# Two mask additions moved from TensorE to VectorE, block means of v in products of their own, and new queues

## Chip, core and metric

The kernel runs on 1 core of one Trainium2 chip. The metric is device time of one execution in microseconds, the median of several runs. The engines are TensorE (PE, with its weight loads as PEld), VectorE (DVE), ScalarE (ACT), GpSimd (POOL) and SyncE (SP), which here issues all transfers. Each engine runs its own queue in order and waits on semaphores for the others.

## What is computed

An attention over a narrow band and block summaries, followed by a GELU MLP, with 4 batches, 8 heads, 768 positions, head dimension 64; d_model 512, d_ff 2048. Inputs and output are f32; the MLP weights arrive as f64.

```python
k_sum = k.reshape(B, H, nb, block, D).max(axis=3)        # block = 32, nb = 24
v_sum = v.reshape(B, H, nb, block, D).mean(axis=3)
scores_l = scale * np.matmul(q, k.transpose(0, 1, 3, 2))
mask_l = np.abs(pos[:, None] - pos[None, :]) < window    # window = 16
scores_s = scale * np.einsum('bhsd,bhnd->bhsn', q, k_sum) + np.log(block)
scores_all = np.concatenate([np.where(mask_l, scores_l, -1e9), scores_s], axis=-1)
a = np.exp(scores_all - scores_all.max(-1, keepdims=True))
a = a / (a.sum(-1, keepdims=True) + 1e-09)
x = np.matmul(a, np.concatenate([v, v_sum], axis=2))     # then heads side by side
h = x @ w_in
out = 0.5 * h * (1 + erf(h / sqrt(2))) @ w_out
```

## The kernel before

The positions are cut into 12 chunks of 256 (`CH`). Attention works in 24 units: one unit is 256 positions of 4 heads (two pairs), so two units feed one chunk of the MLP. A unit's scores are 8 tiles of 128 x 128: the rows are 64 positions of two tiles, the columns a window of 96 keys, 24 block summaries and 8 unused columns.

Units 0 to 5 (batch 0, `WIDE`) are the f32 units, in which the start-up consists. Their products run in f32, straight from what is loaded: `scores` multiplies q by windows of k (`kp0`, 96 columns) and by block maxima (`ks32`, 24 columns), which `prep_k` takes on DVE out of a load of two pairs of heads. The band mask and log(32) are put into PSUM ahead of the scores by `f_mask`, eight products with unit matrices, and the scores accumulate on them. `maximum_p` (DVE) takes row maxima out of PSUM, `exponent_p` (ACT) the exponentials. Units 0 to 2 (`TURNED`) also turn the probabilities on PE in f32 (`p_turn`, kept by ACT's `p_keep`), and multiply them by v in f32 (`values`, 16 products of 64 x 64, in which the block means stand as 24 further rows of v). The means come from `sum_vt` (six products with an indicator) and `mean_vt` (ACT), and `s_load_vs` (ACT) copies them into rows 96 to 119 of each unit's v. From unit 3 on probabilities and v are split in two f16 parts, and the probabilities are turned by DMA (`turn`).

The MLP splits each operand into a high and a low f16 part (three products for one). `w_in` is loaded in 8 column tiles, `w_out` in 8 row tiles, all as f64. Three DVE instructions (`wh_bits`, `wi_bits`, `wo_bits`; the first for half a tile) put together the f32 value, ACT makes the high part (`wi_hi`, `wo_hi`) and DVE the low part (`wi_lo`, `wo_lo`). `take_hi` and `take_lo` do the same for x. `phase1` is a tile of x @ w_in for one chunk (`phase1h` half of its depth), `gelu`, `g_hi`, `g_lo` work on its result, `phase2` is the second product; from chunk 4 on Strassen-like sums of blocks (`product`, `s_product`) take their place. The last PE steps are `s_last`, the last ones on ACT and SP `s_end`.

The order is written out by hand: `ORDER` is a list of some 1,650 steps, each of which issues its instructions on one engine, so the order of each engine's queue is the order of its steps in the list. `warm` steps are products of ones that feed nothing. Of the four banks and rings that steps share, those that matter here are the accumulators `ps_s` (scores of all units but unit 1) and `ps_v` (values), the five PSUM banks, and the single f32 v buffer of units 0, 2 and 3.

Of the kernel before, what the change touches and what calls it, by code (L numbers as in the profile page):

```python
# [80 lines left out]
wh_bits 6 0 2, wh_bits 1 0 0, warm 1 1, f_mask 2, scores 2, maximum_p 2, p_turn 0 1, p_turn 0 0, sum_vt 0,
wi_hi 6 0, exponent_p 2, p_keep 0 1, mean_vt 0, p_keep 0 0, s_load_vs 0, recip 1, wh_bits 1 0 1, p_norm 1,
wi_lo 6 0, wi_bits 4 0, wh_bits 1 0 2, wi_hi 1 0, wi_lo 6 1, wi_bits 4 1, recip 2, wi_bits 4 2, s_norm 2,
p_turn 1 0, p_turn 1 1, f_mask 3, scores 3, values 0, p_keep 1 1, p_keep 1 0, take_hi 0, maximum_p 3, wi_lo 1 0,
sum_vt 1, p_turn 2 1, p_turn 2 0, mean_vt 1, exponent_p 3, s_load_vs 1, wi_bits 0 0, wi_bits 0 1, take_lo 0,
wi_bits 0 2, phase1h 0 6 0, phase1h 0 1 0, f_mask 4, values 1, wi_bits 2 0, wi_bits 2 1, load_q 4, fetch_wh 7 1,
recip 3, wi_hi 4 1, wi_hi 4 0, wi_hi 0 0, wi_bits 2 2, wi_hi 2 0, take_hi 1, wh_bits 7 1 0, scores 4, load_q 5,
load_v 2, fetch_wh 7 0, fetch_w_in 3, fetch_w_out 4, p_keep 2 1, p_keep 2 0, s_load_vs 2, wi_hi 2 1, wi_lo 4 0,
wh_bits 7 1 1, take_lo 1, phase1h 0 4 0, wi_lo 4 1, wi_lo 2 0, p_norm 3, phase1h 0 6 1, values 2, load_v 3,
s_p_hi 3, turn 3 0, wi_lo 0 0, maximum_p 4, wi_lo 2 1, wh_bits 7 0 0, wi_bits 3 0, wh_bits 7 0 1, p_lo 3, take_hi 2,  # L90
# [20 lines left out]
phase2 0 0, phase2 0 1, phase2 1 0, phase2 1 1, phase2 1 5, phase2 1 4, phase2 0 4, phase2 0 5, phase2 0 3,
phase2 0 2, phase2 1 2, phase2 0 6, phase2 0 7, values 5, k_sums 1 1, take_hi 5, scores 6, take_lo 5, add_mask 6,
maximum 6, s_q_hi 8, store 0 0, store 0 1, s_k_hi 7, k_lo 7, phase2 1 6, phase2 1 3, scores 7, q_lo 8, prep_v 1 0,
load_k 8, load_v 6, fetch_v 1 1, exponent 6, recip 6, s_q_hi 9, s_k_hi 8, s_norm 6, s_p_hi 6, add_mask 7, q_lo 9,
k_lo 8, maximum 7, exponent 7, phase1 2 0, phase1 2 4, scores 8, phase1 2 5, phase2 1 7, load_k 9, load_q 10,
gelu 2 4, gelu 2 0, gelu 2 5, g_hi 2 5, s_q_hi 10, s_k_hi 9, g_hi 2 4, fetch_k 2 0, turn 6 0, prep_v 1 1, load_vs 6,
put 0 1, load_q 11, load_k 10, p_lo 6, add_mask 8, recip 7, t_add 1 0, maximum 8, prep_k 2 0, t_add 0 1, phase1 2 1,
phase1 2 3, v_hi 6, store 1 1, gelu 2 1, s_k_hi 10, gelu 2 3, g_hi 2 1, k_lo 9, scores 9, s_q_hi 11, turn 6 1,
v_lo 6, p_norm 7, g_lo 2 5, prep_k_end 2 0, g_lo 2 1, values 6, g_hi 2 0, take_hi 6, s_p_hi 7, g_hi 2 3, exponent 8,
fetch_v 3 0, load_v 7, fetch_v 3 1, load_k 11, put 1 1, load_vs 7, turn 7 0, phase1 2 7, phase1 2 6, gelu 2 6,  # L120
g_lo 2 0, take_lo 6, phase2 2 1, phase1 2 2, prep_v 3 0, q_lo 10, g_lo 2 3, phase2 2 0, t_add 1 1, p_lo 7,
add_mask 9, g_lo 2 4, turn 7 1, k_lo 10, t_add 2 1, recip 8, s_k_hi 11, v_hi 7, v_lo 7, k_lo 11, gelu 2 7,
store 1 0, s_norm 8, values 7, take_hi 7, scores 10, gelu 2 2, s_p_hi 8, phase2 2 5, take_lo 7, maximum 9,
load_q 12, load_v 8, put 0 0, prep_v 3 1, q_lo 11, t_add 1 2, p_lo 8, exponent 9, s_q_hi 12, q_lo 12, recip 9,
p_norm 9, fetch_k 2 1, turn 8 0, load_k 12, load_vs 8, turn 8 1, fetch_v 2 0, phase1 3 3, gelu 3 3, add_mask 10,
g_hi 2 2, g_lo 2 2, g_hi 2 7, v_hi 8, phase1 3 1, gelu 3 1, s_p_hi 9, phase1 3 2, k_sums 2 0, g_hi 3 1, g_hi 2 6,
v_lo 8, load_v 9, load_q 13, put 1 0, load_k 13, phase1 3 0, values 8, scores 11, p_lo 9, turn 9 0, load_vs 9,
phase1 3 5, phase2 2 2, phase2 2 4, phase2 2 3, t_add 0 2, maximum 10, gelu 3 2, s_k_hi 12, k_lo 12, t_add 0 3,
exponent 10, prep_k 2 1, add_mask 11, maximum 11, s_k_hi 13, x_take 8, g_lo 2 7, k_lo 13, exponent 11, v_hi 9,
g_lo 2 6, recip 10, p_norm 10, prep_k_end 2 1, phase2 2 6, v_lo 9, recip 11, gelu 3 0, s_p_hi 10, g_hi 3 0,  # L130
s_norm 11, sx_hi 2 0, s_q_hi 13, g_hi 3 2, turn 9 1, fetch_v 2 1, values 9, prep_v 2 0, prep_v 2 1, x_take 9,
store 2 0, load_k 14, load_q 14, load_v 10, load_vs 10, turn 10 0, g_lo 3 0, p_lo 10, scores 12, phase1 3 4,
phase1 3 7, phase1 3 6, turn 10 1, load_k 15, t_add 2 2, g_lo 3 1, sx_lo 2 0, t_add 1 3, g_lo 3 2, q_lo 13,
gelu 3 5, g_hi 3 5, v_hi 10, g_hi 3 3, g_lo 3 3, k_sums 2 1, s_k_hi 14, gelu 3 4, g_hi 3 4, gelu 3 6, add_mask 12,
v_lo 10, product 2 0 1, phase2 3 1, values 10, scores 13, s_q_hi 14, t_hi 0 0, s_p_hi 11, p_lo 11, t_hi 0 1,
# [1207 lines left out]
```

## Time and profile before

| | |
|---|---|
| median of 3 runs | 549.82 us (549.75 to 550.33) |
| the profiled execution's own time | 549.92 us |
| its span, first to last instruction | 548.1 us |
| busy: PE, DVE, ACT | 539.9, 452.8, 429.7 us |
| mean granted TensorE clock | 0.999 of full speed |
| DMA moved | 74.90 MB, 137 GB/s over the span |

Times of the trace count from the start of the span; the rest of the execution (1.8 us) lies around it. A busy time is a sum over records, and one engine's records may overlap, so two starts that follow on one another say what an instruction takes of its engine's time.

### The profile page before, as it was taken

The page shows a single profiled execution, that of the slowest core. Times are in us where ns is not written, and L with a number is a line of the kernel's source. Part 1 is how long each engine was busy: PE and PEld are TensorE (multiplying, and loading weights), DVE is VectorE, ACT ScalarE, POOL GpSimd, SP SyncE. Part 2 cuts the span into 40 slices and gives each one's busy share as a digit, 9 for nine tenths or more (in the row PEclk, how much of TensorE's full clock was granted, in tenths as well). Part 3 has the DMA queues.
Part 4 walks back from the last instruction along what each step waited for, and adds up shares of the span by engine and source line. Part 5 has one row for each costly group of instructions (what it writes and reads, how often), then busy time and mean ns, then how long its engine had stood idle before and what let it go on. Part 6 is the DMA issues. An engine that isn't in the chain of part 4 may idle for free.

```text
span 548.1 us, 14376 instructions
## 1 busy us (share of the span) xinstructions
PE 539.9 (98%) x6049; PEld 401.0 (73%) x6049; DVE 452.8 (83%) x638; ACT 429.7 (78%) x1009; POOL 0.8 (0%) x9
## 2 busy tenths in 40 slices
PE   9799999999999999999999999999999999999997
PEld 4688884447877675687665787756677888888886
DVE  5999999999989988989879674885889999987411
ACT  3998967859999998899999999998877656655300
POOL 0000000000000000000000000000000000000000
PEclk9999999999999999999999999999999999999999
DMA  8997675597989645472554643434330000100021
GB/s 329 408 381 195 212 242 166 172 287 198 246 224 215 174 122 157 115 200 60 121 153 109 166 80 76 105 99 118 62 69 1 1 20 1 39 2 1 11 67 59
DMA packets 73633, 74.90 MB, mean 137 GB/s; under 512 B 46944, under 2 KB 52960, under 8 KB 73568
## 3 DMA queue, kind: packets, MB, share of 16 engines
q1 hardware_dynamic: 73568, 73.99, 47.2%
q8 instruction: 47, 0.77, 0.6%
q14 instruction: 18, 0.15, 0.1%
HBM read 54.90 MB, written 6.29 MB: 112 GB/s over the span
## 4 chain that ended last, share of the span: by engine, by line
PE 95%; DMA 2%; DVE 2%; issue 0%; ACT 0%; SPq 0%; ACTq 0%
PE bank L1017 27%; PE bank L1080 10%; PE bank L1081 10%; PE bank L1082 10%; PE bank L1194 10%; PE ps_v L923 4%; PE bank L976 4%; PE bank L989 4%; PE bank L977 4%; PE bank L978 4%; PE ps_s L793 3%; PE ps_s L1194 2%; PE ps_v L1194 2%; DMA stage<-in_w_in_dram 1%; PE ps_s L775 1%; DMA w_out_l<-in_kp_first_dram 1%
## 5 line engine op out<-in xcount | busy, mean ns | idle before, releaser
L1080 PE MATMUL bank<-w_out_h,gh 128*128 128x512 f16 x256 | 97.1, 379 | 0.0
L1081 PE MATMUL bank<-w_out_l,gh 128*128 128x512 f16 x256 | 97.0, 379 | 0.0
L1082 PE MATMUL bank<-w_out_h,gl 128*128 128x512 f16 x256 | 97.0, 379 | 0.0
L1017 PEld LDWEIGHTS <-w 128*128 128x128 f16 x640 | 62.5, 98 | 9.3
L1017 PEld LDWEIGHTS <-w_in 128*128 128x128 f16 x576 | 55.9, 98 | 9.2
L1067 DVE SCALAR_TENSOR_TENSOR gl<-g,gh 128x512 f16<-128x512 f32 x76 | 51.4, 685 | 5.9 <-ACT gh L1063 5.9
L833 ACT ACTIVATE s<-s,s_top 128x128 f32<-128x128 f32 x144 | 55.6, 390 | 0.3 <-DVE s_top L810 0.2
L1029 DVE TENSOR_TENSOR g<-bank,late 128x512 f32<-128x512 f32 x48 | 32.9, 685 | 20.4 <-PE bank L1017 9.5
L1063 ACT ACTIVATE gh<-g 128x512 f16<-128x512 f32 x76 | 45.9, 624 | 2.0 <-PE bank L1081 1.4
L1082 PEld LDWEIGHTS <-gl 128*128 128x128 f16 x256 | 25.0, 98 | 30.2
L1017 PE MATMUL bank<-x,w_in 128*128 128x256 f16 x384 | 47.1, 273 | 0.0
L1080 PEld LDWEIGHTS <-gh 128*128 128x128 f16 x256 | 25.0, 98 | 26.7
L1081 PEld LDWEIGHTS <-gh 128*128 128x128 f16 x256 | 25.1, 98 | 26.2
L1017 PE MATMUL bank<-stage,w 128*128 128x256 f16 x320 | 43.6, 273 | 0.0
L1017 PE MATMUL bank<-x,w 128*128 128x256 f16 x320 | 43.4, 273 | 0.0
L1023 ACT ACTIVATE late<-bank 128x512 f32<-128x512 f32 x48 | 28.1, 588 | 19.2 <-PE bank L1017 14.7
L976 PE MATMUL bank<-x,w_in 128*128 128x256 f16 x144 | 39.3, 273 | 0.0
L978 PE MATMUL bank<-x,w_in 128*128 128x256 f16 x144 | 39.3, 273 | 0.0
L977 PE MATMUL bank<-x,w_in 128*128 128x256 f16 x144 | 39.3, 273 | 0.0
L1049 ACT ACTIVATE g<-g 128x512 f32<-128x512 f32 x48 | 29.4, 624 | 9.1 <-DVE g L1029 9.0
L870 ACT ACTIVATE s<-s,s_rec 128x128 f32<-128x128 f32 x104 | 31.7, 390 | 2.1 <-DVE s_rec L848 2.1
L1049 ACT ACTIVATE g<-bank 128x512 f32<-128x512 f32 x48 | 27.9, 590 | 6.5 <-DVE gl L1067 2.1
(242 smaller groups left out, 1242.1 us busy)
## 6 DMA issues: line engine op xcount, KB each, us to landing
v<-in_vw_dram SPq DMA_DIRECT2D x23, 512.0 KB
stage<-in_w_out_dram SPq DMA_DIRECT2D x8, 1024.0 KB
q<-in_qd_dram SPq DMA_DIRECT2D x24, 256.0 KB
k<-in_kd_dram SPq DMA_DIRECT2D x18, 320.0 KB
out_dram<-ot SPq DMA_DIRECT2D x22, 256.0 KB
stage<-in_vb_dram SPq DMA_DIRECT2D x6, 768.0 KB
stage<-in_kp_dram SPq DMA_DIRECT2D x4, 768.0 KB
stage<-in_w_in_dram SPq DMA_DIRECT2D x4, 512.0 KB
```

The source lines that it names most:

```text
L833: nc.scalar.activation(self.s32[:, gs], score[:, ss], AF.Exp, bias=self.top[:, g : g + 1], scale=scale, accum_out=self.den[:, g : g + 1],)
L976: nc.tensor.matmul(dst, wh, xh, start=(k == 0), stop=False)
L977: nc.tensor.matmul(dst, wh, xl, start=False, stop=False)
L978: nc.tensor.matmul(dst, wl, xh, start=False, stop=(k == NCC - 1))
L1017: nc.tensor.matmul(dst, l, r[:, k], start=(first and e == 0 and k == 0 and n == 0), stop=(k == KH - 1 and n == 2), skip_group_check=True,)
L1049: nc.scalar.activation(g, h, AF.Gelu, scale=1.0 / (SC_X * SC_WI))
L1063: nc.scalar.activation(gh, two(g_slot(c, i)), AF.Copy, scale=SC_G)
L1067: nc.vector.scalar_tensor_tensor(out=gl, in0=two(g_slot(c, i)), scalar=SC_G, in1=gh, op0=ALU.mult, op1=ALU.subtract)
L1080: nc.tensor.matmul(t, gh[:, f, js], w_out_h[:, f, :], start=(n == 0), stop=False)
L1081: nc.tensor.matmul(t, gh[:, f, js], w_out_l[:, f, :], start=False, stop=False)
L1082: nc.tensor.matmul(t, gl[:, f, js], w_out_h[:, f, :], start=False, stop=(n == NFC - 1))
L1194: nc.tensor.matmul(acc[:, t * NH : (t + 1) * NH], a[:, f, js], b[:, f], start=(first and j == 0 and t == 0 and f == 0 and n == 0), stop=(f ...
```

## The change

Units 4 and 5 get no `f_mask`: their scores start fresh in PSUM, and DVE adds a mask in f32 (`add_mask`, from a new tile `wide_sb` of 128 KB, loaded by `load_wide`), takes the maximum from SBUF (`maximum` in place of `maximum_p`) and ACT the exponentials from SBUF. Their summary products write 32 columns in place of 24, so that the unused columns are defined. In units 0 to 2 the block means are no longer rows of v: `values_wide` multiplies 96 rows of v by the probabilities as before (16 products), and adds four f32 products of the 24 means with 256 columns each; `s_load_vs` of these units goes, and that of units 3 to 5 stays. v of batch 0 is loaded with 96 rows (384 KB) in place of 128 (512 KB). k of batch 0 comes in four loads, a pair of heads each (400 KB), in place of two of 864 KB, and its block maxima in four DVE steps of half the size. In `scores_wide` the eight window products of a pair come first, then its eight summary products. ORDER is a new list over the whole program.

The engines' instruction counts that differ: PE loses 8 products of 64 x 512 and 8 of 64 x 4 x 24 and gains 12 of 64 x 256; DVE gains 2 additions of 128 x 1024 and loses 2 scalings of 128 x 8, and takes k's maxima in 4 instructions for 2; ACT loses 3 copies of 24 x 1024 and 4 of its 26 table loads, and takes 16 of its exponentials from SBUF.

```diff
-fetch_k 0 0, load_m16, load_q 0, fetch_k 0 1, load_eye, load_q 1, fetch_wh 6 1, fetch_wh 1 1, warm 2 9, warm 3 3,
...
+fetch_kq 0, fetch_kq 1, load_m16, load_q 0, fetch_kq 2, fetch_kq 3, fetch_wh 1 0, load_q 1, prep_kq 0, warm 0 12,
...
-    SP = S + 96
+    SP = S + 2 * WINDOW
...
+    wide_sb = room_h[:, NTT * DM : NTT * DM + 2 * P]
...
+    def load_wide():
+        nc.sync.dma_start(out=wide_sb, in_=mask[:, NMT * TQ + P + NIND :])
...
     def setup():
         nc.gpsimd.memset(ones, 1.0)
+        nc.gpsimd.memset(v32[0][WIDE_SUM:], 0.0)
+        nc.gpsimd.memset(nc_pad, 0.0)
...
-        if b == 0:
-            nc.sync.dma_start(out=kp0[:, rs], in_=kp_first[rs].rearrange("r p s -> p r s"))
-            kst[b, g] = kp0[:, rs, WINDOW : WINDOW + S]
-            return
...
+    def fetch_kq(r):
+        nc.sync.dma_start(out=kp0[:, r], in_=kp_first[r])
+
+    def prep_kq(r):
+        nc.vector.tensor_reduce(
+            out=ks32[:, r], in_=kp0[:, r, WINDOW : WINDOW + S].rearrange("p (n j) -> p n j", j=BLOCK), axis=AX.X, op=ALU.max,
+        )
...
         def load_v(self):
-            nc.sync.dma_start(out=self.v32, in_=vw[self.u].rearrange("p (n j) -> p n j", j=D))
+            rows = slice(0, P if self.b else WIDE_SUM)
+            nc.sync.dma_start(out=self.v32[rows], in_=vw[self.u, rows].rearrange("p (n j) -> p n j", j=D))
...
         def scores_wide(self):
             r0, c0 = self.h0 // 2, self.t0 * TQ
+            sums, pad = ks_flat, 0 if self.masked else P - WIDE_SUM - NBLK
             pse = [self.ps(e) for e in range(2)]
-            for g in range(NG // 2):
-                r, t2 = g // 2, g % 2
-                for part in range(2):
+            for r in range(NR):
+                for part, t in ((part, t) for part in range(2) for t in range(CT)):
+                    g, c = r * CT // 2 + t // 2, t % 2
                     for e in range(2):
-                        for c in range(2):
...
+                            start=not self.masked, stop=(not self.masked or g == NG // 2 - 1 and part == 1),
...
         def add_mask(self):
-            m = self.masks(mask_sb, 2 * NR)
+            m = wide_sb[:, : 2 * P if self.edge else P].unsqueeze(1).broadcast_to([P, UH * (1 if self.edge else 2), 2 * P if self.edge else P]) if self.wide else self.masks(mask_sb, 2 * NR)
...
+        def values_wide(self):
+            for i in range(NR * CT):
+                r, t = divmod(i, CT)
+                for e in range(2):
+                    nc.tensor.matmul(
+                        ps_v[e * D : (e + 1) * D, i * TQ : (i + 1) * TQ], self.v32[:WIDE_SUM, (t * NR + r) * 2 + e, :],
+                        pt32[:WIDE_SUM, e * QCOLS + i * TQ : e * QCOLS + (i + 1) * TQ], start=(i == 0), stop=False, skip_group_check=True,
+                    )
+            rows = slice(WIDE_SUM, WIDE_SUM + NBLK)
+            for r in range(NR):
+                for e in range(2):
+                    h, cs = self.h0 + 2 * r + e, slice(r * CH, (r + 1) * CH)
+                    nc.tensor.matmul(
+                        ps_v[e * D : (e + 1) * D, cs], vm0[rows, h * D : (h + 1) * D],
+                        pt32[rows, e * QCOLS + r * CH : e * QCOLS + (r + 1) * CH], start=False, stop=True, skip_group_check=True,
+                    )
```

Three places show how the queues change. First SP at the very start of the program: the loads of before (kp_first is k of batch 0, mask 128x664 the f16 mask tile, mask 128x128 the unit matrix, qd a unit's q, w_in a half or a whole column tile, vt the v from which the means come).

```order
L546 DMA w_out_l<-in_kp_first_dram 128x2x864
L373 DMA misc<-in_mask_dram 128x664
L672 DMA q_0_83<-in_qd_dram 128x512
L546 DMA w_out_l<-in_kp_first_dram 128x2x864
L379 DMA misc<-in_mask_dram 128x128
L672 DMA q_1_84<-in_qd_dram 128x512
L456 DMA stage<-in_w_in_dram 128x2x512
L456 DMA gl_107<-in_w_in_dram 128x2x512
L672 DMA q_0_83<-in_qd_dram 128x512
L456 DMA stage<-in_w_in_dram 128x2x512
L456 DMA gl_107<-in_w_in_dram 128x2x512
L592 DMA w_out_h<-in_vt_dram 128x2x768
```

And of the change, the same place (a mask row of 128x272 is the unit matrix with the indicator):

```order
L558 DMA w_out_l<-in_kp_first_dram 128x800 x2
L374 DMA misc<-in_mask_dram 128x664
L684 DMA q_0_83<-in_qd_dram 128x512
L558 DMA w_out_l<-in_kp_first_dram 128x800 x2
L462 DMA gl_107<-in_w_in_dram 128x2x512
L684 DMA q_1_84<-in_qd_dram 128x512
L462 DMA stage<-in_w_in_dram 128x2x512
L684 DMA q_0_83<-in_qd_dram 128x512
L462 DMA stage<-in_w_in_dram 128x2x512
L383 DMA misc<-in_mask_dram 128x128
L377 DMA w_out_h<-in_mask_dram 128x272
L604 DMA w_out_h<-in_vt_dram 128x2x768
```

k comes in four pieces, of which two stand ahead of the first q load, and with 800 columns each for 864. The first half tile of weights to come is now one of tile 1 (into gl) and the second one of tile 6 (into stage), before the other way round; each goes one place up against the third q load, which stays behind two of them. The unit matrix, which `p_turn` reads, goes from fifth to tenth place.

Second, DVE from the reciprocals of unit 0 to the maximum of unit 2 (two rows into s_top_98 and their scaling are the maxima of unit 1; rows of 128x512 or 2x256 are weight steps). Before, with the maximum of unit 2 as the last row:

```order
L402 TENSOR_SCALAR w_1_76<-gl_107 128x512
L407 SCALAR_TENSOR_TENSOR w_1_76<-gl_107,w_1_76 128x512
L402 TENSOR_SCALAR w_2_77<-stage 128x512
L411 SCALAR_TENSOR_TENSOR w_1_76<-gl_107,w_1_76 128x512
L821 TENSOR_REDUCE s_top_98<-bank_66 128x4
L821 TENSOR_REDUCE s_top_98<-bank_67 128x4
L825 TENSOR_SCALAR s_top_98<-s_top_98 128x8
L407 SCALAR_TENSOR_TENSOR w_2_77<-stage,w_2_77 128x512
L421 SCALAR_TENSOR_TENSOR w_in_72<-w_1_76,w_in_72 128x2x256
L411 SCALAR_TENSOR_TENSOR w_2_77<-stage,w_2_77 128x512
L402 TENSOR_SCALAR w_1_76<-gl_107 128x512
L810 TENSOR_REDUCE s_top_95<-ps_s 128x8
```

Of the change, from the same step to the same:

```order
L408 TENSOR_SCALAR w_2_77<-stage 128x512
L833 TENSOR_REDUCE s_top_98<-bank_64 128x4
L833 TENSOR_REDUCE s_top_98<-bank_65 128x4
L837 TENSOR_SCALAR s_top_98<-s_top_98 128x8
L413 SCALAR_TENSOR_TENSOR w_2_77<-stage,w_2_77 128x512
L408 TENSOR_SCALAR w_2_77<-stage 128x512
L417 SCALAR_TENSOR_TENSOR w_2_77<-stage,w_2_77 128x512
L413 SCALAR_TENSOR_TENSOR w_2_77<-stage,w_2_77 128x512
L822 TENSOR_REDUCE s_top_95<-ps_s 128x8
```

Eight weight steps stand in the first piece and five in the second. Ahead of both pieces DVE has the same work (block maxima of k, the maximum of unit 0, three bit steps, the reciprocals), and behind both the scaling, one weight step, the reciprocals of unit 1 and `p_norm 1`. So `p_norm 1` has twelve weight steps ahead of it before, and nine in the change.

Third, PE from the end of unit 3's scores to the first product of phase 1. Before (the row into ps_v is `values 0`, 120x256 `sum_vt 1`, bank<-misc,s rows `p_turn 2`):

```order
L775 MATMUL ps_s<-misc,q_1_84 64x24 x4
L775 MATMUL ps_s<-w_out_l,q_1_84 64x96 x4
L775 MATMUL ps_s<-misc,q_1_84 64x24 x4
L923 MATMUL ps_v<-pt,v_0_85 64x64 x16
L597 MATMUL bank_64<-w_out_h 120x256 x6
L876 MATMUL bank_66<-misc,s_0_90 128x128 x4
L876 MATMUL bank_65<-misc,s_0_90 128x128 x4
```

Of the change (64x256 rows are the new products with the means; the rows with q_0_83 are the scores of unit 4, without `f_mask` ahead of them):

```order
L787 MATMUL ps_s<-misc,q_1_84 64x24 x8
L931 MATMUL ps_v<-pt,v_0_85 64x64 x16
L939 MATMUL ps_v<-pt,w_out_l 64x256 x4
L888 MATMUL bank_63<-misc,s_0_90 128x128 x4
L888 MATMUL bank_67<-misc,s_0_90 128x128 x4
L609 MATMUL bank_66<-w_out_h 120x256 x6
L787 MATMUL ps_s<-w_out_l,q_0_83 64x96 x8
L787 MATMUL ps_s<-misc,q_0_83 64x32 x8
L787 MATMUL ps_s<-w_out_l,q_0_83 64x96 x8
L787 MATMUL ps_s<-misc,q_0_83 64x32 x8
L931 MATMUL ps_v<-pt,v_hl_114 64x64 x16
L939 MATMUL ps_v<-pt,w_out_l 64x256 x4
```

`p_turn 2` now stands ahead of `sum_vt 1`, and unit 4's scores and unit 1's values stand ahead of all of phase 1, where before two half tiles of phase 1 came next.

## Rows read from the trace of the kernel before

**Rows 1.** The page of the profiled execution: busy time of each engine, share of the span.
```profile
PE 539.9 (98%) x6049; PEld 401.0 (73%) x6049; DVE 452.8 (83%) x638; ACT 429.7 (78%) x1009; POOL 0.8 (0%) x9
```

**Rows 2.** The page: shares of the chain that ended last, by engine.
```profile
PE 95%; DMA 2%; DVE 2%; issue 0%; ACT 0%; SPq 0%; ACTq 0%
```

**Rows 3.** Stages: busy us (instructions) of PE, PEld, DVE, ACT, POOL; PEclk; DMA share, GB/s.
```profile
15.00:30.00 15.00, 12.04 (x183) 10.21 (x176) 14.48 (x26) 13.74 (x52) 0.00 (x0) 1.00 1.04 406
...
45.00:60.00 15.00, 15.00 (x232) 13.01 (x231) 14.77 (x20) 13.16 (x31) 0.00 (x0) 1.00 0.85 260
...
100.00:150.00 50.00, 50.00 (x579) 32.54 (x578) 48.24 (x61) 41.11 (x104) 0.00 (x0) 1.00 0.84 222
```

**Rows 4.** Timeline of PE: start us, us, line, operation, count, [idle before <- releaser].
```profile
7.05 0.31 PE L775 MATMUL ps_s<-misc,q 64*64 64x24 f32 x8 [0.22 <-DVE misc L556]
...
19.43 2.85 PE L597 MATMUL bank<-w_out_h 128*120 128x256 f32 x12 [1.84 <-ACT s L833]
23.40 2.02 PE L876 MATMUL bank<-misc,s 128*128 128x128 f32 x16 [1.11 <-DVE s L865]
```

**Rows 5.** Chain that ended last, from 20 us: start us, us, what ran (records).
```profile
25.42 0.55 PE ps_s L731 x4
...
26.17 1.25 PE ps_s L775 x64
27.43 1.08 PE ps_v L923 x32
28.51 2.78 PE bank L597 x12
```

**Rows 6.** Timeline of DVE, 4 to 24 us.
```profile
5.24 1.75 DVE L556 TENSOR_REDUCE misc<-w_out_l 128x48 f32<-128x1536 f32 x1 [5.24 <-DMA w_out_l<-in_kp_first_dram]
8.28 1.23 DVE L810 TENSOR_REDUCE s_top<-ps_s 128x8 f32<-128x1024 f32 x1 [1.28 <-PE ps_s L775]
...
9.61 1.75 DVE L556 TENSOR_REDUCE misc<-w_out_l 128x48 f32<-128x1536 f32 x1
...
15.35 0.43 DVE L402 TENSOR_SCALAR w<-stage 128x512 int32<-128x512 int32 x1 [0.86 <-DMA stage<-in_w_in_dram]
...
17.69 0.69 DVE L407 SCALAR_TENSOR_TENSOR w<-stage,w 128x512 int32<-128x512 int32 x1
18.29 0.68 DVE L421 SCALAR_TENSOR_TENSOR w_in<-w,w_in 128x512 f16<-128x512 f32 x1
...
22.04 1.22 DVE L865 TENSOR_TENSOR s<-s,s_rec 128x1024 f32<-128x1024 f32 x1
23.17 0.68 DVE L421 SCALAR_TENSOR_TENSOR late<-w,late 128x512 f16<-128x512 f32 x1
```

**Rows 7.** Timeline of ACT, 9 to 27 us.
```profile
9.81 0.37 ACT L833 ACTIVATE s<-ps_s,s_top 128x128 f32<-128x128 f32 x1 [7.58 <-DVE s_top L814]
...
13.72 2.43 ACT L870 ACTIVATE s<-s,s_rec 128x128 f32<-128x128 f32 x8
...
25.81 1.05 ACT L699 ACTIVATE v<-w_out_l 24x1024 f32<-24x1024 f32 x1
```

**Rows 8.** Timeline of PEld (TensorE weight loads), 0 to 40 us.
```profile
14.09 0.21 PEld L775 LDWEIGHTS ps_s<-w_out_l,q 64*64 64x64 f32 x8 [0.46 <-DMA q<-in_qd_dram]
```

**Rows 9.** DMA, 5 to 40 us: packets, bytes and mean rate.
```profile
DMA packets 6429, 14.18 MB, mean 405 GB/s; under 512 B 407, under 2 KB 700, under 8 KB 6423
```

**Rows 10.** Groups of DVE instructions by form: count, busy us, mean ns, idle before.
```profile
L802 DVE SCALAR_TENSOR_TENSOR s<-ps_s,misc 128x1024 f32<-128x1024 f32 x18 | 21.9, 1214 | 0.9 <-PE ps_s L793 0.6
```

**Rows 11.** Timeline of DVE, 48 to 56 us.
```profile
52.80 0.69 DVE L935 SCALAR_TENSOR_TENSOR x<-ps_v,x 128x512 f16<-128x512 f32 x1 [0.20 <-ACT x L932]
53.41 1.22 DVE L411 SCALAR_TENSOR_TENSOR k<-stage,k 128x1024 int32<-128x1024 int32 x1
```

**Rows 12.** Chain that ended last, from 530 us.
```profile
539.18 5.25 PE bank L1194 x48
...
544.51 0.38 ACT ot L1230
```

More of the change, by code (lines that the diff above doesn't have):

```diff
@@ L81 @@
[L81 to L90, printed above, removed]
@@ L111 @@
[L111 to L120, printed above, removed]
@@ L121 @@
[L121 to L135, printed above, removed]
@@ new lines @@
+wi_lo 1 0, maximum_p 3, wi_bits 2 2, exponent_p 3, fetch_wh 7 0, load_v 1, fetch_w_in 0, fetch_wh 7 1, load_q 5,
+load_v 2, p_turn 2 0, p_turn 2 1, sum_vt 1, scores 4, p_keep 1 1, mean_vt 1, p_keep 1 0, wi_lo 4 0, wh_bits 1 1 0,
+take_lo 0, wh_bits 1 1 1, wh_bits 7 0 0, wh_bits 1 1 2, wi_lo 6 0, recip 3, wh_bits 7 0 1, add_mask 4, p_norm 3,
+values 1, wi_hi 1 1, take_hi 1, wi_hi 4 1, wi_hi 2 0, s_p_hi 3, p_keep 2 0, p_keep 2 1, wi_hi 2 1, wi_hi 6 1,
+fetch_w_out 4, fetch_w_in 3, phase1h 0 1 0, phase1h 0 4 0, phase1h 0 6 0, take_lo 1, maximum 4, wh_bits 7 1 0,
@@ new lines @@
+phase2 0 4, phase2 1 5, phase2 0 5, values 4, warm 1 1, s_norm 5, g_hi 1 7, take_hi 4, s_p_hi 5, g_lo 0 6, g_lo 0 7,
+p_lo 5, prep_k_end 1 0, take_lo 4, g_lo 1 7, load_k 6, load_q 8, load_k 7, turn 5 0, turn 5 1, s_k_hi 6, k_sums 1 0,
+k_lo 6, phase2 1 3, phase2 0 2, phase2 0 3, phase2 1 2, phase2 0 7, prep_k 1 1, v_lo 5, scores 6, add_mask 6,
+prep_k_end 1 1, maximum 6, phase2 1 7, values 5, store 0 1, s_q_hi 8, s_k_hi 7, fetch_v 1 0, put 0 1, load_k 8,
+fetch_v 1 1, k_lo 7, t_add 2 0, take_hi 5, k_sums 1 1, phase2 1 6, prep_v 1 0, exponent 6, recip 6, take_lo 5,
@@ new lines @@
+g_lo 2 1, t_add 2 1, prep_v 3 0, t_add 3 0, exponent 8, load_v 7, put 1 1, load_q 11, load_k 10, load_q 10,
+load_vs 7, turn 7 0, turn 7 1, take_hi 6, v_hi 7, phase1 2 2, phase1 2 6, scores 9, take_lo 6, recip 8, v_lo 7,
+g_lo 2 4, fetch_k 2 1, store 0 0, load_v 8, load_vs 8, put 0 0, load_k 11, values 7, gelu 2 7, g_hi 2 5, take_hi 7,
+add_mask 9, take_lo 7, s_k_hi 10, gelu 2 2, s_q_hi 10, g_hi 2 2, s_norm 8, s_p_hi 8, phase2 2 1, phase1 3 1, v_hi 8,
+s_q_hi 11, g_hi 2 7, gelu 3 1, s_k_hi 11, g_hi 3 1, t_add 3 1, maximum 9, g_lo 2 5, t_add 2 2, t_add 1 1,
@@ new lines @@
+g_lo 3 5, prep_kx 3 0, gelu 3 7, s_norm 11, sx_lo 2 0, k_lo 13, s_q_hi 13, phase2 2 7, phase2 2 6, phase2 3 0,
+put 1 0, turn 10 0, load_vs 11, s_k_hi 14, gelu 3 6, t_hi 0 0, s_q_hi 14, store 2 1, x_take 9, g_hi 3 7, store 2 0,
+g_hi 3 6, k_sums 2 1, s_p_hi 11, product 2 0 1, phase2 3 1, v_hi 11, q_lo 13, g_lo 3 2, add_mask 12, g_lo 3 3,
+maximum 12, values 10, scores 13, x_take 10, q_lo 14, load_q 15, put 2 1, turn 11 0, k_lo 14, p_lo 11, turn 11 1,
+load_k 16, v_lo 11, load_v 12, load_k 15, put 2 0, load_vs 12, add_mask 13, t_lo 0 0, g_lo 3 6, maximum 13,
```

323 lines of the change are left out of this document (171 added, 152 removed).

## The prediction

> **What bounds the kernel now.** I read the page's busy times first: TensorE is busy for 539.9 of 548.1 us, VectorE for 452.8, ScalarE for 429.7 [rows 1], and the chain that ended last is 95% PE [rows 2]. So time can be won in two ways: PE gets less to do, or PE waits less. Next I asked the timeline of PE where it waits. The last two waits are in the start-up: 1.84 us ahead of `sum_vt 0` at 19.43, and 1.11 us, ended by DVE's `p_norm 1`, ahead of `p_turn 1` at 23.40 [rows 4]. From 23.40 on PE follows PE without a gap, through the stages [rows 3] to the last product, which starts at 539.18 and takes 5.25 us; behind that is a tail of ACT and store from 544.51 on [rows 12]. The edits leave this tail alone.
>
> So the program has two parts. Up to 23.40 us it is a race of loads and of DVE. Behind it every microsecond of PE work counts, if DVE keeps up. That is not sure: DVE is busy for 14.48 of 15 us from 15 to 30 us, 14.77 from 45 to 60 and 48.24 of 50 from 100 to 150 [rows 3]. It runs beside PE with nothing to spare, and the change gives it more.
>
> **The start, up to `p_turn 1`.** What is late there is `p_norm 1`, from 22.04 to 23.17 by starts [rows 6], at the end of a DVE queue that hardly idles. Three things take time out of that queue.
>
> First, the loads. They come at 405 GB/s from 5 to 40 us, 395 KB per us [rows 9]. The scores of unit 0 waited for the block maxima of k [rows 4], which DVE takes from 5.24, when 864 KB of k are there, to 6.99 [rows 6]. The change has half of this k, 400 KB, 464 KB earlier: 464/395 is 1.2 us, so DVE starts at 4.1, takes the halves as they land and ends at 6.0. The scores then wait for q, behind 64 KB less than before, and I put the maximum of unit 0, which starts at 8.28 [rows 6], at 7.72.
>
> Second, the 0.86 us wait of DVE for a weight load at 15.35 [rows 6] goes. Ahead of the same load stand four k loads of 400 KB in place of two of 864, so about 0.3 us fewer bytes; and DVE asks for it later, as its first half tile is another one. I estimate its landing at 14.9 and DVE's demand at 15.25. The third q load lands at 14.09 before [rows 8] and, with 192 KB fewer ahead of it, at 13.6.
>
> Third, `p_norm 1` has nine weight steps of 512 columns ahead of it instead of twelve. From 17.69 to 18.29 one takes 0.60 us [rows 6], so three are 1.8. Together 0.56 + 0.86 + 1.8 = 3.2 us at most. A walk through the queue checks it, each step by its row (a maximum with its scaling 1.33, 8.28 to 9.61; a pair of block maxima 1.75, `p_norm` 1.22 [rows 6]): unit 0's maximum to 9.05, block maxima to 10.8, three weight steps to 12.6, the reciprocals (0.3) to 12.9, one step to 13.25, unit 1's maxima to 14.65, four steps (with at most a short wait for the half tile) to 16.8, unit 2's maximum to 18.1, one step and the reciprocals to 19.05, `p_norm 1` to 20.25. ScalarE's 2.43 for unit 0 [rows 7] and an exponential at 0.37 lie beside that. `p_turn 1` then starts at 20.4. I take **-3.0 us**. PE has done the same work by then in both, but for one row of fillers, `warm 1 1`, which the change runs later, among work that counts: **+0.2**. The bounds of the first term: 0 if the loads don't follow the bytes, -4 if DVE's small waits vanish too.
>
> **The masks of units 4 and 5.** PE loses two `f_mask`. One lasts from 25.42 to 26.17, its first four products alone 0.55 [rows 5]: 2 x 0.75 = **-1.5 us**. DVE gains two `add_mask` of 128 x 1024; the same form from PSUM stands with a mean of 1.21 us over 18 [rows 10], and the maximum from SBUF is taken at the price of the one from PSUM, 1.23 [rows 6]. So DVE gets about 2.3 us more, since by starts a step of 1024 columns is 1.13 (22.04 to 23.17 [rows 6]). I cost that at nothing on PE, because units 4 and 5 are scored well ahead of their use; the cover is PE's own queue. If it is gone, up to 2.3 us come back. By running sums of rows the closest place is the first low part of x and of `w_in` for phase 1, some 25 to 55 us in: DVE is there 0.9 to 1.3 us ahead of PE, about what it was in the kernel before (there `take_lo` at 52.80 to 53.41 [rows 11], with phase 1 of the chunk at about 53.4). The wider summaries of these units, 32 columns for 24, and the regrouped `scores_wide` (1.25 us for 64 records, two for each product [rows 5]) I leave at nothing, bounds -0.1 and +0.1 a unit.
>
> **The block means.** Three units lose a 24-row copy of 1.05 us on ACT [rows 7], which is off the chain once PE is full, and gain four f32 products of 256 columns on PE. The trace has no such product, so I bound it. In the 16 products of `values 0` (32 records) two that write different halves of PSUM's partitions run side by side: 16 x 64 columns in 1.08 us [rows 5]. Four products of 256 have the same 1024 columns, and by that row cost 1.0, or 0.85 if nothing but columns counted. The other end is `sum_vt`, six products of 256 columns which don't pair, 2.78 us or 0.463 each [rows 5]: 4 x 0.463 = 1.85, and 0.11 for a change of tile shape is 1.96. (The 0.11: 48 products of 256 columns in f16 take 5.25 us [rows 12], so 512 columns 0.219; the four products of `f_mask`, of 512 columns, as two pairs would be 0.44, and they take 0.55 [rows 5].) Since the new ones write halves just as those of `values` do, they are nearest to that row: 3 x 1.0 = **+3.0 us**. The bounds are +2.6 and +5.9.
>
> At this point a rule speaks against the change. `f_mask` takes 0.11 us more than its columns, beside products of another shape [rows 5]. The Trainium skill, "TensorEngine Tiling (Array Packing)", section Key Properties, says that switching the tiling mode drains TensorE. By the row three such switches are 0.33 us, which lie inside the 3.0 (3 x 0.85 would be 2.55); the page doesn't size a drain, so by it the sum stays the same.
>
> **The rest of the list.** ORDER moves steps over the whole program. Behind 75 us PE has at least 8 us of margin to DVE and ACT by running sums, and the products are the same; I put that at nothing, bounds -0.3 and +0.5.
>
> **The sum**, against the profiled execution's 549.92 us: its span is 548.1, with 1.8 around it, and it lies 0.1 above the median of 549.82. -3.0 - 1.5 + 3.0 + 0.2 = -1.3 us, so 548.6.
>
> **Rivals.**
> - *The new products don't pair.* Then three units cost 5.9, and the sum is -3.0 - 1.5 + 5.9 + 0.2 = +1.6: 551.5, slower. It decides from about 1.8 us a unit on. Against it: their addresses are halves as in `values`, which pairs. For it: they read rows 96 to 119 only, and share these rows. Chance 0.15.
> - *DVE falls behind.* The added 2.3 us use up the margin of about 1 us between 40 and 75 us, PE waits 1.5 us there, and 550.1 comes out: no change. For it: DVE's 14.77 of 15 [rows 3]. Against it: the start gives DVE its 0.86 us of waiting back, so of the 2.3 us only 1.4 are new up to there. Chance 0.2.
> - *The start gains half.* If loads of 400 KB come later than their bytes say, `p_norm 1` waits for a load as before, and of 3.0 only 1.5 remain: 550.1. The row for it is the 405 GB/s [rows 9], which smaller and larger loads of before share. The Trainium skill, "DMA: Bandwidth & Descriptors", section Bandwidth, asks for loads of 1 MiB or more to get three quarters of the peak, which speaks against quarter loads; the trace reaches its 405 GB/s with loads mostly below that. Chance 0.12.
> - *More than forecast.* Products at 0.85, `p_turn 1` at 19.4: 547.1. Chance 0.13.
>
> **How the numbers follow.** What remains, 0.4, is the forecast, 548.6, with its own range of 547.8 to 549.4. About 0.2%, 1.1 us, is what a measurement of this kernel can tell from no change: faster is below 548.7, slower above 550.9. Faster holds two thirds of the forecast's chance, 0.27, the whole of the last case, 0.13, and 0.05 of the second and third rivals: 0.45. Slower is the first rival and 0.05 of the second, for a wait longer than 1.5 us: 0.2. What remains, 0.35, is no change. The range, 546.9 to 551.3, holds the last case and nearly reaches the first.
>
> **What the profile would show.** Right: `p_turn 1` starts at 20.4 us or so on PE, and no idle time of PE follows; the rows of 64 x 256 products take 1.0 us a unit; no `f_mask` row in units 4 and 5; the two additions on DVE wait for PE and no PE row waits for them. Wrong: PE rows with an idle time ended by DVE between 25 and 75 us (second rival), a weight or q load that ends DVE's or PE's wait at 13 to 17 us (third), about 1.9 us a unit in the new products (first). The prediction would fall as a whole if the new list opened a wait in the Strassen part, where I looked only at sums.

## The result, and the profile after

The changed kernel takes 553.87 us, median of 4 runs (552.84 to 554.39); the kernel before took 550.08 beside it (549.75 to 550.55, 4 runs). The ratio is 1.0068, with a 95% interval of 1.0053 to 1.0083: it is 0.7% slower, where 548.6 was forecast with a range up to 551.3. The profiled execution took 553.77 us, with a span of 552.0.

Busy times first (the row of before is in [rows 1]):

```profile
PE 542.7 (98%) x6057; PEld 401.7 (73%) x6057; DVE 455.5 (83%) x640; ACT 419.9 (76%) x1002; POOL 1.8 (0%) x11
```

PE is still busy for 98%, so the page alone hides what happened. The timeline of PE shows its waits from `p_turn 1` on. Start and duration in us, line, operation, count, and in brackets the idle time before and what ended it:

```profile
21.36 2.02 PE L888 MATMUL bank<-misc,s 128*128 128x128 f32 x16 [0.55 <-DVE s L877]
...
24.93 0.56 PE L787 MATMUL ps_s<-w_out_l,q 64*64 64x96 f32 x16 [0.80 <-DMA q<-in_qd_dram]
26.57 1.15 PE L931 MATMUL ps_v<-pt,v 96*64 96x64 f32 x32 [0.32 <-DMA v<-in_vw_dram]
...
41.73 1.15 PE L931 MATMUL ps_v<-pt,v 96*64 96x64 f32 x32 [0.95 <-DMA v<-in_vw_dram]
...
155.06 0.92 PE L954 MATMUL ps_v<-pt,v_hl 128*64 128x64 f16 x46 [1.61 <-DMA pt<-p_l]
```

`p_turn 1` starts at 21.36 in place of 23.40 [rows 4]: the start gains 2.04 us. Then come four waits of a kind that the kernel before didn't have from there on, each ended by a transfer, 3.68 us in all. The rest I worked out by adding up, from `p_turn 1` on, the times from one product's start to the next one's, by function, in both traces: the missing `f_mask` give 1.43 back, the values of units 0 to 2 cost 3.12 more, `warm 1 1` 0.32, and 0.4 is spread over the rest. -2.04 - 1.43 + 3.12 + 0.32 + 0.4 + 3.68 = +4.05, and that is what the end shows: the last step on ACT starts at 548.56, in place of 544.51 [rows 12].

The chain of waits from 28 to 45 us leads to one load (start, duration, what):

```profile
28.10 13.50 DMA v<-in_vw_dram
41.60 0.14 issue
41.73 1.15 PE ps_v L931 x32
42.89 1.01 PE ps_v L939 x8
```

The v load of unit 2, 384 KB, is issued at 28.10 and lands 13.5 us later, the time behind earlier loads included. The last row shows the new products at the forecast price, 1.01 us a unit. By stages of the start (busy us and instructions of PE, PEld, DVE, ACT, POOL, then PEclk, DMA share, GB/s):

```profile
15.00:21.00 6.00, 5.41 (x60) 4.43 (x54) 5.86 (x12) 6.00 (x31) 0.00 (x0) 1.00 1.05 406
21.00:26.00 5.00, 3.84 (x84) 3.21 (x85) 4.90 (x8) 4.11 (x16) 0.00 (x0) 1.00 1.06 275
26.00:30.00 4.00, 3.68 (x72) 2.97 (x65) 3.97 (x7) 3.54 (x14) 0.00 (x0) 1.00 1.06 402
30.00:36.00 6.00, 5.98 (x119) 5.08 (x119) 4.51 (x11) 4.14 (x17) 0.00 (x0) 1.00 1.04 291
36.00:42.00 6.00, 5.05 (x53) 3.95 (x51) 6.00 (x8) 5.21 (x12) 0.00 (x0) 1.00 1.04 301
```

Here is the cause to look for: the DMA engines are busy all the time (share 1.04 to 1.06), and yet they move 275 to 301 GB/s in three of five stretches, where the kernel before held 405 over 5 to 40 us [rows 9]. They are occupied, not idle. In the last of the stretches the kernel before moved no more, but for another reason: its engines had less to do (share 0.74).

```profile
36.00:42.00 6.00, 6.00 (x146) 5.20 (x144) 6.00 (x9) 5.48 (x10) 0.00 (x0) 1.00 0.74 295
```

The three stretches are those in which a v load of batch 0 lands: by the completions in the trace the parts of the three loads come in at 23.2 to 26.5, 31.2 to 34.5 and 38.4 to 41.6.

### The profile page after: what moved, and what is told of

Read it like the earlier page. It is cut to its first block, busy times and chain, and to the rows that moved or that the text cites. A ratio compares the mean times of both kernels' runs of the same rounds, so it can differ in the third digit from the quotient of the medians.

```text
span 552.0 us, 14401 instructions
## 1 busy us (share of the span) xinstructions
PE 542.7 (98%) x6057; PEld 401.7 (73%) x6057; DVE 455.5 (83%) x640; ACT 419.9 (76%) x1002; POOL 1.8 (0%) x11
## 4 chain that ended last, share of the span: by engine, by line
PE 90%; DMA 8%; ACT 1%; DVE 0%; issue 0%; SPq 0%; ACTq 0%; POOL 0%; POOLq 0%
PE bank L1048 27%; PE bank L1111 10%; PE bank L1113 10%; PE bank L1112 10%; PE bank L1225 9%; DMA v<-in_vw_dram 6%; PE ps_v L954 3%; PE bank L1020 3%; PE bank L1007 3%; PE bank L1008 3%; PE bank L1009 3%; PE ps_s L805 2%; PE ps_s L1225 2%; PE ps_v L1225 2%; DMA q<-in_qd_dram 1%; PE bank L996 1%
## 5 line engine op out<-in xcount | busy, mean ns | idle before, releaser
L845 ACT ACTIVATE s<-s,s_top 128x128 f32<-128x128 f32 x160 | 61.8, 389 | 1.2 <-DVE s_top L822 1.1
```

The lines of the kernel that those rows point to most:

```text
L845: nc.scalar.activation(self.s32[:, gs], score[:, ss], AF.Exp, bias=self.top[:, g : g + 1], scale=scale, accum_out=self.den[:, g : g + 1],)
```

## The experiments

**The rows of a load, alone in the old kernel.** Its edit, with the rows from 96 on zeroed once:

```diff
-            nc.sync.dma_start(out=self.v32, in_=vw[self.u].rearrange("p (n j) -> p n j", j=D))
+            rows = slice(0, P if self.b else WIDE_SUM)
+            nc.sync.dma_start(out=self.v32[rows], in_=vw[self.u, rows].rearrange("p (n j) -> p n j", j=D))
```

> The kernel before with one part of the change alone: v of batch 0 in loads of 96 rows (384 KB in place of 512); rows 96 on are zeroed once at the start. Theory A: 96 rows are slow whatever the order is, so the DMA rate of 15 to 42 us falls from about 400 GB/s to under 300 while they are in flight, the load of w_out that landed at 42.0 lands 2 to 4 us later although 384 KB fewer are moved, and TensorE waits somewhere between 25 and 60 us: 550.5 to 552. Rival B: fewer bytes, earlier loads: the last one lands about 1 us earlier, at 41, and the time stays at 550.1.

Measured: 550.38 us, ratio 1.0005 (0.9996 to 1.0013). The rate fell:

```profile
21.00:26.00 5.00, 3.89 (x35) 2.83 (x36) 4.97 (x10) 4.85 (x21) 0.00 (x0) 1.00 1.03 341
26.00:30.00 4.00, 4.00 (x104) 3.65 (x102) 3.93 (x8) 3.98 (x12) 0.00 (x0) 1.00 1.08 373
30.00:36.00 6.00, 6.00 (x53) 4.98 (x51) 5.90 (x9) 5.90 (x22) 0.00 (x0) 1.00 1.04 297
```

By the completions in the trace the load of w_out lands at 45.3 in place of 42.0, though 384 KB fewer were moved by then. So the load by 96 rows is slow in the old order too, as theory A has it. But no PE row behind 24 us waits for a load: in the old order what is loaded has 3 us to spare. Theory A was right on the rate (297 to 373 GB/s, if not under 300 throughout) and wrong on the time.

**The rows of a load, by themselves.** A kernel of loads alone; its edit is the whole program:

> A kernel that only loads, and writes zeros as its output: nine groups of eight loads of 4096 bytes a row from v, with a pause between groups: 128 rows, 96, 64, 112, 64 and 32 in two loads, 128 and 96 by turns, 128 rows of 3200 bytes, 120, 128 again. Theory A: the rate hangs on the count of rows alone; 128 rows run at about 400 GB/s, 96 rows at 220 to 290 by themselves, 96 and 128 by turns no better, and packets of the 96-row loads take 220 to 300 ns in place of 159. Rival B: 96 rows are as fast as 128 when nothing else loads, about 400 GB/s, and it was a collision with other traffic of the kernel. Theory A leaves open what 112 and 120 rows do; if it is a matter of rows that don't divide into equal shares of full groups, 120 and 112 are slow too and 64 and 32 apart are not.

Between two groups DVE writes a column of the target, which waits for all loads of the group. The time from one such write to the next is the time of eight loads, in one execution (timeline of DVE):

```profile
1.88 0.07 DVE L101 MEMSET x<- 128x8 f32 x1
15.65 0.07 DVE L101 MEMSET x<- 128x8 f32 x1 [13.70 <-DMA x<-in_vw_dram]
29.17 0.07 DVE L101 MEMSET x<- 128x8 f32 x1 [13.46 <-DMA x<-in_vw_dram]
41.71 0.07 DVE L101 MEMSET x<- 128x8 f32 x1 [12.47 <-DMA x<-in_vw_dram]
58.19 0.07 DVE L101 MEMSET x<- 128x8 f32 x1 [16.41 <-DMA x<-in_vw_dram]
73.72 0.07 DVE L101 MEMSET x<- 128x8 f32 x1 [15.47 <-DMA x<-in_vw_dram]
88.50 0.07 DVE L101 MEMSET x<- 128x8 f32 x1 [14.71 <-DMA x<-in_vw_dram]
99.91 0.07 DVE L101 MEMSET x<- 128x8 f32 x1 [11.34 <-DMA x<-in_vw_dram]
117.91 0.07 DVE L101 MEMSET x<- 128x8 f32 x1 [17.93 <-DMA x<-in_vw_dram]
132.75 0.07 DVE L101 MEMSET x<- 128x8 f32 x1 [14.77 <-DMA out_dram<-zero]
```

| eight loads of | KB | us, from row to row |
|---|---|---|
| 128 rows | 4096 | 13.77 |
| 96 rows | 3072 | 13.52 |
| 64 rows | 2048 | 12.54 |
| 112 rows | 3584 | 16.48 |
| 64 and 32 rows apart | 3072 | 15.53 |
| 128 and 96 rows by turns | 3584 | 14.78 |
| 128 rows of 3200 bytes | 3200 | 11.41 |
| 120 rows | 3840 | 18.00 |
| 128 rows once more, the last of them beside stores of the output | 4096 | 14.84 |

A quarter of the rows left out saves 0.25 of 13.77 us. Each group's time includes some 3 us up to its first landing. By the completions in the trace (the median of a load's 16 parts) one 96-row load follows another after 1.40 us, and one 128-row load another after 1.32; the first six of the repeat, which have no stores beside them, come 1.30 apart. As theory A expected, single packets, each a row of 4096 bytes, take longer: the median in the trace is 241 ns in the 96-row group and 159 in the 128-row group. Why they do, no run here shows.

112 and 120 rows take longer than 128. And 96-row loads by turns with 128-row loads make the whole group slower than 128-row loads alone, though it moves fewer bytes: they hold up what runs beside them. Fewer bytes in a row do save time: 3200 bytes for 4096 give 11.41. Rival B, that 96 rows are as fast when nothing else loads, is out. Splitting 96 into 64 and 32 doesn't help, against the guess at the end of the expectation.

The Trainium skill, "SBUF — State Buffer", section "Door 1: The DMA port swizzle", says that partitions 0 to 63 reach half of the memory's DMA ports, and gives 196 GB/s for them against 328 for 128. The run agrees in the main: half of the bytes take 12.54 us for 13.77. The page gives no rate for 96, 112 or 120.

**128 rows in the changed kernel.** The load of v as in the kernel before:

```diff
-            rows = slice(0, P if self.b else WIDE_SUM)
-            nc.sync.dma_start(out=self.v32[rows], in_=vw[self.u, rows].rearrange("p (n j) -> p n j", j=D))
+            nc.sync.dma_start(out=self.v32, in_=vw[self.u].rearrange("p (n j) -> p n j", j=D))
```

> The changed kernel, but v of batch 0 comes in 128 rows again (512 KB a load in place of 384). Theory A: the 96-row loads themselves are slow and hold up every load beside them; the changed kernel's DMA rate of 220 to 290 GB/s in stretches between 21 and 42 us goes back to about 400, the three waits of TensorE for q of unit 3 (0.80 us at 24.93), v of unit 0 (0.32 at 26.57) and v of unit 2 (0.95 at 41.73) vanish, and the time is about 551.8 us, 2.1 below the changed kernel. Rival B: the loads are late because the new list issues them late and much stands ahead; then 128 KB more in each of three loads make each wait 0.3 us longer, about 554.8.

Measured: 554.5 us (551.9 to 557.04), ratio 1.008 (1.0054 to 1.0106). In this run and in the one with both edits the load of units 3 to 5 overwrites the block means, which the new list copies ahead of it; the means' part of these units is left out of the output. The three waits went, and the theory's time didn't come: the load of unit 3 now waits for that copy, the transposes stand behind the load, and PE waits 1.93 us for them at 53.59. The edit had brought a wait of its own. The profiled execution takes 556.91: it also waits 1.56 us for the mask at 7.77 and 1.4 for a later transpose, and behind the waits at 7.77 and 53.59 the granted clock is 0.50 for 3.4 us each, the lower of its two levels. So this run decides neither way on the time; the rate, 397 to 415 GB/s up to 36 us, is theory A's. Next, 128 rows for units 0 to 2 alone:

```diff
-            rows = slice(0, P if self.b else WIDE_SUM)
+            rows = slice(0, P if self.b or self.turned else WIDE_SUM)
```

> The changed kernel with 128-row loads of v for units 0 to 2 alone; units 3 to 5 keep their 96 rows, so that their load doesn't wait for the copy of the block means. Theory A (96-row loads hold up all others): the three waits for q of unit 3, v of unit 0 and v of unit 2 vanish, no new wait at 50 us, and the median is 551.8 (2.1 below the changed kernel's 553.87). Rival B (something else in the first 50 us is late next, so that the first waits only move): above 553.

Measured: 550.58 us, ratio 1.0002 (0.9990 to 1.0015), 3.3 us below the changed kernel. The stages in question:

```profile
21.00:26.00 5.00, 4.68 (x112) 4.08 (x114) 4.90 (x8) 4.13 (x16) 0.00 (x0) 1.00 1.05 412
26.00:30.00 4.00, 4.00 (x44) 3.29 (x39) 3.97 (x7) 4.00 (x17) 0.00 (x0) 1.00 1.04 405
30.00:36.00 6.00, 6.00 (x121) 4.72 (x120) 5.97 (x11) 4.10 (x16) 0.00 (x0) 1.00 1.05 412
```

The rate is 405 to 412 GB/s, and PE has no idle row behind 21.32. More bytes, earlier landing: theory A holds, and the gain is larger than its 2.1 since the wait at 155 us is gone too in the profiled execution. That one takes 549.56 us. Five of the twelve executions take 549.4 to 549.7, the other seven 550.5 to 552.63, and what these wait for is not shown.

**The start.** k of batch 0 in two loads, on top of that run:

```diff
-        nc.sync.dma_start(out=kp0[:, r], in_=kp_first[r])
+        if r % 2 == 0:
+            rs = slice(r, r + 2)
+            nc.sync.dma_start(out=kp0[:, rs], in_=kp_first[rs].rearrange("r p s -> p r s"))
```

> The changed kernel with 128-row loads of v for units 0 to 2 (550.58 us), and k of batch 0 in two loads of two pairs (800 KB each) in place of four of 400 KB, at the places of the first and the third. Theory A: the quarter loads are what makes the first transfers ragged (the mask's last sixteenth lands 0.6 to 2.5 us after its median, against 0.2 in the kernel before); with two loads the mask and q land by 5.7 and 6.3, the maximum of unit 0 starts near 8.2 in place of 8.6, the time falls by 0.3 to 0.5, to about 550.2, and the runs lie closer together (before: 1.5 us from lowest to highest; with quarters 3.2). Rival B: the raggedness has another cause; DVE starts 1.2 us later on k, unit 0 gains nothing, and 550.6 or more comes out with the same spread.

Measured: 549.30 us (548.92 to 551.3), ratio 0.9989 (0.9979 to 0.9998), the one version that is faster than the kernel before, by 0.1%. First the changed kernel's DVE, then this run's, at unit 0's maximum:

```profile
8.62 1.23 DVE L822 TENSOR_REDUCE s_top<-ps_s 128x8 f32<-128x1024 f32 x1 [2.38 <-PE ps_s L787]
```

```profile
5.25 1.81 DVE L563 TENSOR_REDUCE misc<-w_out_l 128x24 f32<-128x768 f32 x2 [5.25 <-DMA w_out_l<-in_kp_first_dram]
7.82 1.22 DVE L824 TENSOR_REDUCE s_top<-ps_s 128x8 f32<-128x1024 f32 x1 [0.76 <-PE ps_s L789]
```

DVE begins later on k and has unit 0's maximum 0.8 us earlier (the run that this one is built on has it at 8.59). By the completions in the trace the first q load is there at 6.25 in its last part (7.08 in the run built on, 6.84 in the changed kernel), the medians being 6.04, 6.13 and 6.11. Only 0.44 us of it reach `p_turn 1`, which starts at 20.88 for 21.32; most of the rest goes at 13.27, where DVE now waits 0.20 us for a weight load. The median fell by more, 1.28 us, since nine of twelve executions lie under 549.6 here; why, the profiles, 549.52 and 549.56, don't show. The spread of the runs hardly shrank, 2.4 us for 3.2.

**The wait at 155 us.** SP in the changed kernel, from unit 7's v load (L700) over its block means (L720) to the transposes (L904); the duration is that of the issue:

```profile
141.42 0.34 SPq L700 DMA_DIRECT2D v<-in_vw_dram  x1
...
147.57 1.67 SPq L720 DMA_DIRECT2D v<-misc  x2
149.36 1.26 SPq L904 DMA_TRANSPOSE pt<-p_h  x1
150.66 1.30 SPq L904 DMA_TRANSPOSE pt<-p_l  x1
```

Three edits of the list, the first to the changed kernel, the others to the run with 128 rows for units 0 to 2. Only the steps that move are shown:

```diff
-load_v 7, put 1 1, load_q 11, load_k 10, load_q 10, load_vs 7, turn 7 0, turn 7 1,
+load_v 7, put 1 1, load_q 11, load_k 10, load_q 10, turn 7 0, load_vs 7, turn 7 1,
...
+load_v 7, load_vs 7, turn 7 0, turn 7 1, put 1 1, load_q 11, load_k 10, load_q 10,
...
+load_v 7, put 1 1, load_vs 7, turn 7 0, turn 7 1, load_q 11, load_k 10, load_q 10,
```

> The changed kernel, but on SP the first transpose of unit 7 stands ahead of the copies of its block means, which wait for unit 7's v load. Theory A: the 1.61 us in which TensorE waits at 155.06 for the second transpose of unit 7 come from SP standing still from 144.7 to 147.57 behind that load; with the first transpose issued in this time the second one lands 1.3 us earlier, the wait falls to about 0.3 us, and the time is 552.6. Rival B: TensorE waits next for something else that is late by as much (the low part of x on VectorE, scores of unit 9): 553.9, as the changed kernel.

> As the run before it, and on SP the copies of unit 7's block means and its two transposes stand right behind its v load; a store, two q loads and a k load that stood between go behind them. Theory A: the v load lands some 3 us after its issue in place of 6, the copies go early, and the transposes start as soon as unit 6's products have freed their target; TensorE's wait of 1.61 us ahead of the second part of unit 7's products falls below 0.3 and the median is 1.3 to 1.6 below the run before it, about 550.3. Rival B: what holds the transposes is the target alone; the wait stays at 1.2 us as in the earlier run with one transpose moved, 551.5.

> The changed kernel with 128-row loads of v for units 0 to 2 (550.58 us), and on SP only the two q loads and the k load that stood between unit 7's v load and its copies and transposes go behind them; the store stays ahead. Theory A: in part of the executions the copies wait for a late v load and TensorE for the transposes behind them, up to 1.6 us; with fewer transfers beside it the v load is early, the median falls to 549.5 to 550 and the runs lie closer together. Rival B: the later q and k loads are late in their turn, as the store was when it was moved too: 551 to 552.

Measured: 553.84 us, ratio 1.0070 (1.0048 to 1.0092); 551.81, 1.0036 (1.0023 to 1.0049); 551.12, 1.0018 (1.0009 to 1.0027). None helps. In the first, the transpose waits for PE to be done with unit 6, whose turned probabilities lie in the same place, and PE's wait only falls to 1.20 us. The second takes the wait away and makes another: ACT now waits 4.3 us for a store that went to the back, and PE 1.8 for ACT (the profiled execution, 553.84, is 2 us above the median). Waits of ACT, and of PE, by what ended them (total, times, longest):

```profile
ACT ot L1116 <- DMA out_dram<-ot: 4.3, 1, 4.3
```

```profile
PE bank L1006 <- ACT x L962: 1.8, 1, 1.8
```

The third makes PE wait 1.09 us at 171.0 for ACT, which had waited for a k load and for block means that now come later. The rivals had the times about right in all three, but their reasons only in the third: in the first PE still waits for the same transpose, and in the second it isn't the target that holds it. The first edit joined to the 128-row loads:

> Both edits of the two runs above in one kernel. Theory A: the two waits are apart, so both gains add up: 553.87 - 2.1 - 1.3 = 550.5, the same as the kernel before within 0.2%. Rival B: an earlier start meets a transfer that is no earlier; then the second wait grows by what the first edit gives, and about 552 comes out.

Measured: 553.0 us, ratio 1.0055 (1.0042 to 1.0069); the unit 3 wait of above is in it, 1.42 and 0.63 us, so it says nothing on the sum.

**The block means as rows of v again**, on top of the second edit of the list:

```diff
-            if self.turned:
-                return self.values_wide()
...
-            terms = ((vh, self.ph), (vh, self.pl), (vl, self.ph))
+            terms = ((self.v32, pt32),) if self.turned else ((vh, self.ph), (vh, self.pl), (vl, self.ph))
...
-p_turn 1 1, p_turn 1 0, f_mask 3,
+p_turn 1 1, p_turn 1 0, f_mask 3, s_load_vs 0,
...
-p_keep 1 1, mean_vt 1, p_keep 1 0,
+p_keep 1 1, mean_vt 1, p_keep 1 0, s_load_vs 1,
...
-p_keep 2 0, p_keep 2 1, wi_hi 2 1,
+p_keep 2 0, p_keep 2 1, s_load_vs 2, wi_hi 2 1,
```

> As the run before it, with the block means of units 0 to 2 as rows of v again: the twelve products of 64 x 256 go, and three copies of 1.05 us come back on ScalarE, each as late as it can stand. Theory A: TensorE saves 3 x 1.0 us and waits 0 to 0.8 us for the copies of units 1 and 2, so the time is 1.6 to 3 us below the run before it, 547.5 to 548.7. Rival B: ScalarE is the late one there, the copies push its exponentials and parts back, and the products were the price for that: within 0.5 us of the run before it.

Measured: 552.41 us, ratio 1.0041 (1.0028 to 1.0054), 0.6 above the run that it is built on. PE's waits:

```profile
PE ps_v L951 <- ACT v L711: 1.5, 2, 0.8
PE ps_v L951 <- ACT v_hl L711: 1.3, 1, 1.3
```

The copies cost 2.8 us of waiting where the products cost 3.0 of work: rival B in kind, 0.1 beyond its 0.5. In this order the products are no loss against the copies.

**The masks by products again**, on top of the run with 128 rows for units 0 to 2:

```diff
-scores 4,
+f_mask 4, scores 4,
...
-add_mask 4,
+maximum_p 4,
...
-maximum 4,
...
-exponent 4,
+exponent_p 4,
```

and the same for unit 5.

> The changed kernel with 128-row loads of v for units 0 to 2 (550.58 us), and units 4 and 5 masked by products again: two f_mask come back on TensorE, the two additions on VectorE go. Theory A: VectorE hides the additions completely, so TensorE's 2 x 0.75 us come back: 552.1. Rival B: VectorE is as full as TensorE there and the additions cost what they saved: no change, 550.6.

Measured: 555.38 us, ratio 1.0090 (1.0077 to 1.0103), 4.8 above. Neither theory has that number. PE at unit 5's mask, and the stages behind it:

```profile
43.36 0.62 PE L744 MATMUL ps_s<-misc 128*64 128x512 f16 x4 [1.35 <-ACT s L845]
```

```profile
43.00:44.00 1.00, 0.64 (x8) 0.23 (x7) 1.00 (x3) 0.98 (x3) 0.00 (x0) 0.99 0.77 275
44.00:45.00 1.00, 1.00 (x28) 0.88 (x29) 0.60 (x2) 0.97 (x2) 0.00 (x0) 0.50 1.24 205
45.00:46.00 1.00, 1.00 (x40) 1.00 (x36) 0.96 (x2) 0.97 (x3) 0.00 (x0) 0.50 1.23 255
46.00:47.00 1.00, 1.00 (x26) 0.83 (x20) 0.39 (x1) 1.00 (x2) 0.00 (x0) 0.50 0.67 130
47.00:48.00 1.00, 1.00 (x9) 0.81 (x8) 0.78 (x1) 0.98 (x2) 0.00 (x0) 0.80 0.44 164
```

The sum of starts gives 1.58 us for the two `f_mask`, as theory A has it. The 1.35 us ahead of 43.36 is new: unit 4's scores stay in PSUM until ACT has taken the exponentials, and unit 5 needs the place. `add_mask` had moved them to SBUF. Behind that wait the granted clock is 0.50 for 3.4 us, the lower of its two levels, which costs half of that, 1.7 us. 0.7 us more are waited at 155 to 156, 0.45 for a transpose and 0.22 for DVE; that the masks cause these is not shown. 1.58 + 1.35 + 1.7 + 0.7 = 5.3, of the profiled execution's 5.2 (554.72 against 549.56).

## Why the prediction was wrong

**The loads** are the step that failed. The working priced them by their bytes, 395 KB per us [rows 9], and gave the v loads of batch 0 with 96 rows no term, not even a rival. No row before had a 96-row load of this size at the start. Eight of them take 13.52 us, against 13.77 for eight of 128 rows, and they slow the others. The cost was 2.07 us in three waits of PE; the run that undid it lies 3.3 us lower by the median, the wait at 155 us included. In the old order the same loads cost no time (1.0005): it takes the new order, in which PE needs what they hold up, to make them dear. The third rival had the right kind of failure, loads that come later than their bytes say. It named k's quarters alone; they were late too, as the start shows.

**The rest of the list** was put at nothing, bounds -0.3 and +0.5. The fourth wait, 1.61 us at 155.06, lies there. "At least 8 us of margin" was a sum of engine rows; SP's queue, where a transpose stands behind copies that stand behind a load, was not in it. Why the wait is absent in the profile with 128 rows for units 0 to 2 isn't settled: there the copies follow the load by 4.9 us, not by 6.2, and I didn't find what makes the difference.

**The start** was mis-sized: 2.04 us in place of 3.0. The walk was right from its first step on: from unit 0's maximum to the end of `p_norm 1` it said 12.5 us, and 8.62 to 21.13 is 12.5. The first step was late by 0.9, at 8.62 in place of 7.72. With two loads of k it comes at 7.82, so most of that was the quarter loads' doing; `p_turn 1` is then at 20.88, still 0.5 later than forecast.

**The block means** cost 1.01 us a unit, by pairing as argued; the first rival is out. **The masks** gave 1.43 for 1.5, and DVE hid the additions: no PE row behind 23 us waits for DVE, so the second rival is out. Undoing the masks in the list as it stands costs 4.8 us, more than their price, since with them the scores leave PSUM early. **`warm 1 1`** was 0.32 for 0.2.

Without the 96-row loads of units 0 to 2 the same adding up gives -2.08 for the start, -1.51 for the masks, +2.94 for the values, +0.31 for `warm 1 1` and +0.22 spread, -0.1 in all; that run measured 1.0002. So even with the loads put right the forecast of -1.3 would have been missed, by the start above all.

## What to carry to other kernels

Price a load by its rows as well as by its bytes: leaving out 32 of 128 rows saved 2% of the time here and slowed the loads beside it, leaving out 64 saved 9%, and rows shorter by 22% saved 17%. A busy share of DMA near 1 beside a fallen GB/s is the sign to look for. When steps are reordered, follow each transfer queue to its last wait as the engines' queues are followed, since the margin of the engines says nothing on it.
